# A chunk of weights folded in halves around the second stage, and other chunks' bit work moved behind the steps' copies

## The chip, the core and the metric

The kernel runs on one core of a Trainium2 chip. The metric is the device time of one execution in microseconds. A core has five engines that run side by side, each in its own program order: TensorE (PE) multiplies matrices into PSUM banks, VectorE (DVE), ScalarE (ACT) and GpSimd (POOL) work elementwise, and SyncE (SP) issues most of the DMAs. They wait for one another through semaphores.

## The reference, cut to what matters

```python
def _attn_ref(x):                       # x: (8, 3008, 256)
    X = np.fft.fft(x, axis=1)
    X = np.fft.fft(X, axis=2)
    return X.real.astype(np.float32)

def _moe_ref(x, w_in, w_out):           # w_in (256, 2048), w_out (2048, 256)
    h = x @ w_in
    g = h * (1.0 / (1.0 + np.exp(-1.702 * h)))
    return (g @ w_out).astype(np.float32)
```

The real part of a two-dimensional Fourier transform of each of 8 batches goes through a two-layer network with a sigmoid-type activation. Everything is 32-bit floats.

## The kernel before

The transform along the sequence is split into two stages of matrix products (3008 = 47 x 64). The transform along the 256 features is never done by itself: it is folded into the first weight matrix, `wcs = cd x w_in`, in four chunks of 512 columns (`fold_w(0)` to `fold_w(3)`). The network then runs in 384 steps (8 batches x 3 blocks x 2 halves x 8 pairs of 128 hidden columns). The first eight steps (`t < NP`, NP = 8) go through `hidden`, `rows`, `activate` and, three steps later (`LAG = 3`), `product`; all later ones go through `begin`, `forward`, `backward` and others. Steps 0 and 1 need chunk 0 of the folded weights, steps 2 and 3 chunk 1, and so on.

The weights do not arrive as plain floats: w_in and w_out come as 64-bit words whose bits are turned into 32-bit floats on the chip. Each of the eight chunks, named `("in", n)` or `("out", n)` (`in0`, `in1`, `out0`, `in2` and so on in the text), is loaded into a ring of three raw buffers and goes through these operations, each over 128 x 1024 elements:

- `prepare` takes a buffer each of the rings `s`, `m` and `r`;
- `squares` (L401, ScalarE; for chunk `in0` L403, VectorE) squares the high word, read as a float;
- `clamp` (L406, GpSimd) limits it;
- `low_up` (L411) and `low_down` (L416), both ScalarE, round the low word;
- `high` (L433, L434, L435, VectorE) masks and shifts the clamped word into a buffer of ring `a`;
- `finish_in` (L447, GpSimd) or `finish_out` (L455, two instructions) adds both parts, into `wst` or `wo`.

`bounds(key)` is prepare, squares, clamp, low_up and low_down in a row. A raw buffer is free for the load three places later once its clamp, squares and low_up are done: `load_in(3)` follows `out0`, `load_out(2)` follows `in2`, and `load_out(3)` follows `out1` in that ring.

`fold_w(n)` multiplies both halves of `wst[n]` (i = 0, 1) into two PSUM banks and ScalarE copies them to `wcs` (L474). `first_row(n)` makes two small per-column factors of the chunk by eight tiny products and two ScalarE copies (L482, L483). `rotate` (psr, with a copy at L341) and `stage2` (L354, then VectorE's transposes L360) make the operand `pq` of block 0. `nyquist(0, 0)` makes the row `nb` by a product and a ScalarE copy (L372). `warm` issues a matmul with no use of its result.

In step t < 8, `hidden(t)` multiplies `pq` with two pairs of columns into banks `pa` and `pb`, and ScalarE copies `pa` to `v` (L515); `rows(t)` makes the hidden rows on VectorE (L553, L556 twice, L544); `activate(t - 1)` is one ScalarE instruction (L562).

Program order is the order of each engine: the kernel schedules by hand. Before the steps stands a list of calls; within the steps the dictionary `extra` holds what runs at the end of step t, entered with `at(t, function, ...)`. PSUM banks without a fixed name are handed out in rotation from the list `spare` (six tags); a bank's next user waits for its last reader. At t = NP - 3 = 5, `hidden` takes `b0` and `b1` by name.

The SP queue holds, in order: `load_in(3)` (L383), `load_out(2)` and `load_out(3)` (L388), `load_matrices` (L318), `turn` (L194, L190: part of the next batch is reversed into a DRAM buffer Xr), `load_x` (L203: the next batch, half of it from Xr), and two 4 KB DMAs of zeros into row 0 of `wcs[1]` (L970). The first of these zeros is needed by `begin(8, 1)`, the product into `x` with which TensorE opens step 8.

Of the kernel before, what the change touches and what calls it, by code (L numbers as in the profile page):

```python
# [111 lines left out]
def kernel(ctx: ExitStack, tc, x, w_in, w_out, tab1, tab2, out):  # L112
# [36 lines left out]
    o_banks = [psp.tile([128, 512], F32, tag=f"o{i}", name=f"o{i}") for i in range(2)]  # L149
    rest = psu.enter_context(tc.tile_pool(name="psu", bufs=1, space=PS))  # L150
    big = cv.tile([128, 19 * 1024], F32, tag="big", name="big")
    rings = {"s": (0, 1024, 3), "a": (3072, 1024, 1), "raw": (4096, 2048, 3), "h": (10240, 1024, 4), "r": (14336, 1024, 2),
             "m": (16384, 1024, 2)}
    turns = {}

# [11 lines left out]
    def bank(name, tag=None):  # L167
        if tag is None:
            tag = spare.pop(0)
            spare.append(tag)  # L170
        if tag in ("o0", "o1"):
            return o_banks[int(tag[1])]
        return (rest if tag[0] == "o" else psp).tile([128, 512], F32, tag=tag, name=name)
# [5 lines left out]
    def halves(out, lhs, rhs, **how):  # L179

        for c0 in (0, 64):
            nc.tensor.matmul(out[c0:c0 + 64], lhsT=lhs[:, c0:c0 + 64], rhs=rhs, skip_group_check=True, **how)  # L182
# [137 lines left out]
    def warm(n):  # L320

        ps = bank("warm")
        for _ in range(n):
            nc.tensor.matmul(ps[:], lhsT=wcs[0][:, 0:128], rhs=wcs[0][:, 0:512], start=True, stop=True)
# [11 lines left out]
    def rotate(b, a0=0, a1=NG, copy=None):  # L336

        col = t4t[b][:, a0:a1, H]
        ps = bank("psr")
        halves(ps[:, 0:a1 - a0], rot, col, start=True, stop=True)  # L340
        (copy or nc.vector.tensor_copy)(col, ps[:, 0:a1 - a0])  # L341
# [51 lines left out]
    def prepare(key):  # L393


        pre[key] = ring("s"), ring("m"), ring("r").bitcast(U32)

    def squares(key, eng):
        g, hi = pre[key][0], raw[key][:, :, 1].bitcast(F32)
        if eng is nc.scalar:  # L400
            eng.activation(g[:], hi, ACTF.Square)  # L401
        else:
            eng.tensor_tensor(g[:], hi, hi, op=ALU.mult)  # L403

    def clamp(key, lo=0, n=1024):
        nc.gpsimd.tensor_scalar(pre[key][1][:, lo:lo + n], raw[key][:, lo:lo + n, 1].bitcast(F32), scalar1=TOP, scalar2=-TOP,  # L406
                                op0=ALU.min, op1=ALU.max)

    def low_up(key, lo=0, n=1024):

        nc.scalar.activation(pre[key][2][:, lo:lo + n].bitcast(F32), raw[key][:, lo:lo + n, 0], ACTF.Copy, scale=2.0 ** -29,  # L411
                             bias=2.0 ** 23)
# [12 lines left out]
    def high(key, lo=0, n=1024):  # L425

        g, m, _ = (t[:, lo:lo + n] for t in pre[key])
        bits = m.bitcast(U32)
        if lo == 0:
            made_a[key] = ring("a").bitcast(U32)  # L430
        a = made_a[key][:, lo:lo + n]
        dve = nc.vector
        dve.scalar_tensor_tensor(m, g, LOW * LOW, m, op0=ALU.is_ge, op1=ALU.mult)  # L433
        dve.tensor_scalar(a, bits, scalar1=3, scalar2=0x3FFFFFF8, op0=ALU.logical_shift_left, op1=ALU.bitwise_and)  # L434
        dve.scalar_tensor_tensor(a, bits, 0xC0000000, a, op0=ALU.bitwise_and, op1=ALU.bitwise_or)  # L435
# [5 lines left out]
    def finish_in(n, lo=0, k=1024):  # L441

        if lo == 0:
            wst[n] = op.tile([128, 2, 512], F32, tag="os", name="wst")
        key, part = ("in", n), slice(lo, lo + k)
        out = wst[n][:].rearrange("p i f -> p (i f)")[:, part]
        nc.gpsimd.tensor_tensor(out.bitcast(U32), made_a[key][:, part], pre[key][2][:, part], op=ALU.add)  # L447
# [16 lines left out]
        for out, i0, i1 in ((t1, b12, b11), (t2, b22, t1), (t3, b22, b12), (t4, b21, t2)):  # L464
            nc.gpsimd.tensor_tensor(out, i0, i1, op=ALU.subtract)

    def fold_w(n):
        ps = [bank("psw") for _ in range(2)]
        for i in range(2):
            for cs in range(2):  # L470
                halves(ps[cs][:], cd[:, i, cs, :], wst[n][:, i, :], start=(i == 0), stop=(i == 1))
        for cs in range(2):

            nc.scalar.copy(wcs[cs][:, n * 512:(n + 1) * 512].rearrange("p (f c) -> p f c", f=4),  # L474
                           free(ps[cs][:], 0, [1, 4], [4, 128]))
# [400 lines left out]
        spill_first(k, 16, NM, (nc.sync, nc.sync))  # L876
    prepare(in1)
    squares(in1, nc.scalar)
    for h0 in (0, 512):
        finish_in(0, h0, 512)  # L880
    clamp(in1)
    low_up(in1)
    low_down(in1)
    high(in1)
    load_out(1, nc.sync)
    fill(0, 4, NG)
    warm(1)
    fold_w(0)
    warm(1)
    first_row(0)  # L890
    prepare(out0)
    finish_in(1)
    clamp(out0)
    rotate(0, 0, 4, nc.scalar.copy)
    squares(out0, nc.scalar)
    stage2(0, 0)
    warm(1)
    low_up(out0)
    low_down(out0)
    high(out0)  # L900
    load_in(3, nc.sync)
    prepare(in2)
    squares(in2, nc.scalar)
    clamp(in2)
    fold_w(1)
    finish_out(0)

    extra, early = {}, {}

    def at(t, fn, *args):  # L910
        extra.setdefault(t, []).append((fn, args))

    n = len(steps)

    for t, key in (1, in2), (2, ("out", 1)), (3, ("in", 3)), (5, ("out", 2)), (6, ("out", 3)):
        at(t, high, key)
        if key != in2:
            at(t - 1, bounds, key)
        at(t + 1, finish, key)
    early[3], early[5] = 2, 3  # L920
    rows_at = {1: 1, 4: 2, 6: 3}
    for t, c in ((0, 2), (1, 3)):
        at(t, load_out, c, nc.sync)
    at(3, load_matrices)
    if B > 1:
# [35 lines left out]
    for t in range(n + LAG):  # L961
        if t < NP:
            if t == NP - 3:
                spare[:] = [tag for tag in spare if tag[0] == "o"] + ["b2"]
            hidden(t)
            if t == NP - 1:
                middle(NP)
                begin(NP)
                for c0 in range(0, DF, 1024):
                    nc.sync.dma_start(out=wcs[1][0:1, c0:c0 + 1024], in_=tab1[127:128, n0 + 4:n0 + 1028])  # L970
            if t == 0:
                low_up(in2)
                nyquist(0, 0)
                low_down(in2)
            if t in rows_at:
                first_row(rows_at[t])
            if t >= LAG:
                product(t - LAG, 0, None)
            if t in early:
                fold_w(early[t])  # L980
            if t:
                activate(t - 1)
            rows(t)
            if t == NP - 1:
                doubled(NP)
                middle(NP + 1)
        else:
            after, special = (any(fn in (mix1, stage2) for fn, _ in extra.get(k, ())) for k in (t - 1, t))
            if t < n:
                begin(t, 1)  # L990
            if t == NP:
                activate(t - 1)
            if t < n:
                forward(t)
            if after and t + 1 < n:
                middle(t + 1)
            opening = (t - LAG) % NP == 0 and t >= NP + LAG
            one, other = (t - LAG, (1, 2, 4, 7)), (t - LAG - 1, (5, 6, 3))
            if opening:
                small_products(*other)  # L1000
            cut = 0 if opening and not after else 3 if after else 2
            product(t - LAG, 0, cut)
            if after:
                small_products(one[0], one[1][:1])
                small_products(other[0], () if opening else other[1][:1])
            if t + 1 < n:
                begin(t + 1)
            if not opening:
                small_products(other[0], other[1][after:])
            product(t - LAG, cut, 6 if t - LAG == last else None)  # L1010
            small_products(one[0], one[1][after:])
            swap(t - LAG - 2)
            if t < n:
                backward(t)
            if t + 1 < n:
                doubled(t + 1)
            if t < n:
                activate_back(t)
                sums(t, nc.gpsimd)
            if t + 2 < n and not special:  # L1020
                middle(t + 2)
            combine_small(t - LAG - 1)
            if t - LAG == last:
                product(last, 6, None)
            sums(t - 1, nc.vector)
            deeper(t - 2, 0)
            deeper(t - 3, 1)
        if t == NP:
            psu.close()
            low = ctx.enter_context(tc.tile_pool(name="low", bufs=1, space=PS))  # L1030
            pot["low"] = low.tile([128, 3 * 512], F32, tag="low", name="low")
        if t >= LAG:
            combine(t - LAG)
            combine_last(t - LAG - 2)
            turn_last(t - LAG - 3, 0)
            turn_last(t - LAG - 4, 1)
        if t >= NP:
            spare[:] = [f"b{t % 2}"] * special + ["b2"]
        for fn, args in extra.get(t, ()):
            fn(*args)  # L1040
# [28 lines left out]
```

## Time and profile before

| | us |
|---|---|
| median of 4 runs | 1866.89 (1864.21 to 1868.07) |
| device time of the profiled execution | 1861.57 |
| its span, first to last instruction | 1859.8 |
| TensorE busy in 0 to 25 us | 22.38 |
| in 25 to 36 us (11 us) | 8.92 |
| in 36 to 48, 48 to 60, 60 to 72 us (12 us each) | 12.00, 10.72, 12.00 |
| in 72 to 85 us (13 us) | 11.91 |
| bytes moved in 36 to 48, 48 to 60, 60 to 72, 72 to 85 us | 343, 342, 172, 123 GB/s |

The granted TensorE clock is 1.00 in all these stretches. In the lines of a timeline the first number is the start and the second the duration in microseconds; in brackets stands how long the engine was idle before, and what ended it. A record of 8 or 16 instructions on one line is one run of equal instructions. The DMA share of the stretch from 36 to 60 us is 0.97 to 1.03, from 60 to 85 us 0.82 to 0.86, and from 85 to 97 us 0.01.

### The profile page before, as it was taken

How to read it: one execution, taken by the hardware profiler on the slowest of the kernel's cores; microseconds unless marked ns; L12 is line 12 of the kernel's file. 1: busy time of each engine (PE TensorE's matmuls, PEld its weight loads, DVE VectorE, ACT ScalarE, POOL GpSimd, SP SyncE). 2: the span in 40 equal slices, each digit the busy share in tenths (PEclk: the TensorE clock that was granted, in tenths of full speed). 3: DMA queues.
4: the chain of work that ended last, by engine and by line, in shares of the span. 5: the costliest groups of instructions: out<-in, count | busy, mean ns of one | idle time of the engine just before them, and what ended most of it. 6: DMA issues, size and time to landing. Idle time of an engine off the chain costs nothing.

```text
span 1859.8 us, 55818 instructions
## 1 busy us (share of the span) xinstructions
PE 1843.4 (99%) x23684; PEld 1404.8 (76%) x23684; DVE 1522.7 (82%) x2229; ACT 1149.9 (62%) x2248; POOL 963.4 (52%) x1057
## 2 busy tenths in 40 slices
PE   8999999999999999999999999999999999999998
PEld 5677777777777777777777777777777777778776
DVE  7888788888798877997789878888888888878874
ACT  6656656666656656666665666656666666656663
POOL 5676346744367444773347643476445754434442
PEclk9999999999999999999999999999999999999999
DMA  8720351125120350114402152022511021100111
GB/s 278 181 52 17 83 95 35 30 63 108 24 51 14 82 95 18 51 21 107 68 13 57 39 103 49 18 59 50 104 30 25 19 63 36 31 19 13 22 20 24
DMA packets 145690, 105.29 MB, mean 57 GB/s; under 512 B 105163, under 2 KB 128235, under 8 KB 144258
## 3 DMA queue, kind: packets, MB, share of 16 engines
q1 hardware_dynamic: 144226, 101.20, 25.3%
q8 instruction: 187, 3.06, 0.7%
q10 hardware_dynamic: 1216, 0.52, 0.1%
q14 instruction: 61, 0.50, 0.1%
HBM read 64.41 MB, written 48.05 MB: 60 GB/s over the span
## 4 chain that ended last, share of the span: by engine, by line
PE 87%; DVE 6%; ACT 3%; DMA 2%; POOL 1%; issue 1%; SPq 0%; DVEq 0%; ACTq 0%; POOLq 0%
PE x L182 32%; PE o L182 24%; PE low L664 23%; PE o L664 4%; DVE big L630 2%; PE ps L354 1%; PE ps L253 1%; DVE big L765 1%; DVE big L544 1%; DMA wcs<-in_tab_dram 1%; ACT x L571 1%; DMA big<-in_moe_w_in_dram 1%; ACT big L586 0%; ACT xt L256 0%; ACT g L583 0%
## 5 line engine op out<-in xcount | busy, mean ns | idle before, releaser
L601 POOL TENSOR_TENSOR big<-big 128x256 f32<-128x256 f32 (+1 forms) x376 | 349.6, 930 | 840.5 <-ACT big L593 790.0
L182 PE MATMUL x<-pq,wcs 128*64 128x256 f32 (+1 forms) x6016 | 771.4, 377 | 3.6 <-ACT g L583 2.2
L630 DVE TENSOR_TENSOR big<-big 128x512 f32<-128x512 f32 (+1 forms) x736 | 636.6, 879 | 30.9 <-PE low L664 14.0
L182 PE MATMUL o<-big,wo 128*64 128x256 f32 (+1 forms) x4800 | 621.1, 375 | 0.0
L182 PEld LDWEIGHTS x<-pq,wcs 128*64 128x64 f32 x6016 | 410.0, 137 | 193.8 <-issue 15.6
L182 PEld LDWEIGHTS o<-big,wo 128*64 128x64 f32 x4800 | 341.8, 137 | 146.7 <-DVE big L608 0.5
L583 ACT ACTIVATE g<-x 128x512 f32<-128x512 f32 (+1 forms) x376 | 221.6, 589 | 372.7 <-PE x L182 371.5
L544 DVE TENSOR_TENSOR big<-g,x 128x512 f32<-128x512 f32 (+2 forms) x440 | 253.7, 588 | 200.5 <-ACT big L586 200.1
L664 PE MATMUL low<-big 128*64 128x128 f32 (+1 forms) x5888 | 381.9, 270 | 0.0
L571 ACT ACTIVATE x<-nb,af 128x256 f32<-128x256 f32 (+1 forms) x752 | 352.7, 469 | 12.2
L664 PEld LDWEIGHTS low<-big 128*64 128x64 f32 x5888 | 337.1, 137 | 28.7
L602 POOL TENSOR_TENSOR big<-big 128x256 f32<-128x256 f32 (+1 forms) x376 | 358.6, 954 | 0.0
L586 ACT ACTIVATE big<-x 128x512 f32<-128x512 f32 (+1 forms) x376 | 220.5, 586 | 196.4 <-PE x L182 180.5
L593 ACT ACTIVATE big<-big 128x512 f32<-128x512 f32 (+1 forms) x376 | 231.8, 617 | 41.8 <-DVE big L544 40.0
L664 PE MATMUL low<-big,wo 128*64 128x128 f32 (+1 forms) x2944 | 220.2, 270 | 0.2 <-DVE big L630 0.2
L664 PEld LDWEIGHTS low<-big,wo 128*64 128x64 f32 x2944 | 171.9, 137 | 3.8 <-DVE big L630 0.4
L609 DVE TENSOR_TENSOR big<-big 128x512 f32<-128x512 f32 (+1 forms) x188 | 147.7, 786 | 6.5
L608 DVE TENSOR_TENSOR big<-big 128x512 f32<-128x512 f32 (+1 forms) x188 | 136.6, 727 | 5.4 <-POOL big L601 5.4
L765 DVE TENSOR_TENSOR big<-big,low 128x512 f32<-128x512 f32 (+3 forms) x184 | 109.0, 609 | 3.5
L664 PEld LDWEIGHTS o<-big,wo 128*64 128x64 f32 x1472 | 92.3, 137 | 24.9
L664 PE MATMUL o<-big,wo 128*64 128x128 f32 (+1 forms) x1472 | 110.1, 270 | 0.0
L225 POOL TENSOR_TENSOR xt<-xt 111x510 f32<-111x510 f32 x56 | 77.1, 1377 | 4.4
(102 smaller groups left out, 965.2 us busy)
## 6 DMA issues: line engine op xcount, KB each, us to landing
out_dram<-os SPq DMA_DIRECT2D x284, 64.0 KB
t<-Td SPq DMA_DIRECT2D x22, 512.0 KB
Td<-xt SPq DMA_DIRECT2D x14, 768.0 KB
xt<-in_x_dram SPq DMA_DIRECT2D x14, 512.0 KB
xt<-Xr SPq DMA_DIRECT2D x14, 512.0 KB
nb<-Nd SPq DMA_DIRECT2D x23, 256.0 KB
out_dram<-os SPq DMA_DIRECT2D x96, 56.0 KB
Xr<-in_x_dram SPq DMA_DIRECT2D x7, 752.0 KB
```

Of the source, the lines that this page charges most:

```text
L182: nc.tensor.matmul(out[c0:c0 + 64], lhsT=lhs[:, c0:c0 + 64], rhs=rhs, skip_group_check=True, **how)
L544: nc.vector.tensor_tensor(free(out, at + m - 1, [by, 2], [RUN, blocks], [-1, m]), *ins, op=op)
L571: nc.scalar.activation(x[:, i * 256:i * 256 + n], nbt[b, blk][:, hh * 256:hh * 256 + n], ACTF.Copy, scale=af1[:, f:f + 1])
L583: nc.scalar.activation(two(g[:], n), two(xb[t][:], n), ACTF.Copy, scale=2.0)
L586: nc.scalar.activation(front(t), two(xb[t][:], width(t)), ACTF.Gelu_apprx_sigmoid)
L593: nc.scalar.activation(back(t), back(t), ACTF.Gelu_apprx_sigmoid)
L601: eng.tensor_tensor(right(t, S1, n), left(t, A21, n), right(t, A22, n), op=ALU.add)
L602: eng.tensor_tensor(left(t, S3, n), left(t, A11, n), left(t, A21, n), op=ALU.subtract)
L608: eng.tensor_tensor(s2, s1, a11, op=ALU.subtract)
L609: eng.tensor_tensor(s4, a12, s2, op=ALU.subtract)
L630: nc.vector.tensor_tensor(out, i0, i1, op=how)
L664: nc.tensor.matmul(o, lhsT=lhs, rhs=rhs, start=first_in, stop=(p == NP - 2), skip_group_check=True)
```

## The change

`fold_w` can now do one half at a time; the chain of clamp, finish and fold of chunk `in1` is cut into halves, and `fold_w(1)` is placed around `rotate` and `stage2`. Two of the three `warm(1)` calls ahead of the steps are left out. `low_up` and `low_down` of `out0`, and `squares`, `low_up` and `low_down` of `in2`, move into steps 0 and 1; `finish_out(0)` and `finish(in2)` move to the end of step 1, the bounds of `out1` from step 1 to step 2, and `load_out(2)` and `load_out(3)` each one step later. Ring `a` of masked words has two buffers instead of one, ring `s` two instead of three.

```diff
-    rings = {"s": (0, 1024, 3), "a": (3072, 1024, 1), "raw": (4096, 2048, 3), "h": (10240, 1024, 4), "r": (14336, 1024, 2),
+    rings = {"s": (0, 1024, 2), "a": (2048, 1024, 2), "raw": (4096, 2048, 3), "h": (10240, 1024, 4), "r": (14336, 1024, 2),
...
-    def fold_w(n):
-        ps = [bank("psw") for _ in range(2)]
-        for i in range(2):
+    folded = {}
+
+    def fold_w(n, parts=(0, 1)):
+        if parts[0] == 0:
+            folded[n] = [bank("psw") for _ in range(2)]
+        ps = folded[n]
+        for i in parts:
             for cs in range(2):
                 halves(ps[cs][:], cd[:, i, cs, :], wst[n][:, i, :], start=(i == 0), stop=(i == 1))
+        if parts[-1] == 0:
+            return
...
     squares(in1, nc.scalar)
-    for h0 in (0, 512):
-        finish_in(0, h0, 512)
+    finish_in(0, 0, 512)
     clamp(in1)
+    finish_in(0, 512, 512)
     low_up(in1)
     low_down(in1)
-    high(in1)
+    for h0 in (0, 512):
+        high(in1, h0, 512)
     load_out(1, nc.sync)
     fill(0, 4, NG)
     warm(1)
     fold_w(0)
-    warm(1)
+    prepare(out0)
+    for h0 in (0, 512):
+        finish_in(1, h0, 512)
+    clamp(out0)
+    fold_w(1, (0,))
+    rotate(0, 0, 4, nc.scalar.copy)
+    stage2(0, 0)
+    squares(out0, nc.scalar)
+    fold_w(1, (1,))
     first_row(0)
-    prepare(out0)
-    finish_in(1)
-    clamp(out0)
-    rotate(0, 0, 4, nc.scalar.copy)
-    squares(out0, nc.scalar)
-    stage2(0, 0)
-    warm(1)
-    low_up(out0)
-    low_down(out0)
     high(out0)
-    load_in(3, nc.sync)
     prepare(in2)
-    squares(in2, nc.scalar)
     clamp(in2)
-    fold_w(1)
-    finish_out(0)
...
-    for t, key in (1, in2), (2, ("out", 1)), (3, ("in", 3)), (5, ("out", 2)), (6, ("out", 3)):
+    at(1, finish_out, 0)
+    at(1, high, in2)
+    at(1, finish, in2)
+    at(2, bounds, ("out", 1))
+    for t, key in (2, ("out", 1)), (3, ("in", 3)), (5, ("out", 2)), (6, ("out", 3)):
         at(t, high, key)
-        if key != in2:
+        if t > 2:
             at(t - 1, bounds, key)
         at(t + 1, finish, key)
...
-    for t, c in ((0, 2), (1, 3)):
+    for t, c in ((1, 2), (2, 3)):
         at(t, load_out, c, nc.sync)
...
             if t == 0:
-                low_up(in2)
                 nyquist(0, 0)
-                low_down(in2)
+                low_up(out0)
+                load_in(3, nc.sync)
+            if t == 1:
+                low_down(out0)
             if t in rows_at:
                 first_row(rows_at[t])
+            if t == 1:
+                squares(in2, nc.scalar)
+                low_up(in2)
+                low_down(in2)
```

## The prediction

> **What bounds the kernel now.** I read four views, in this order. The page first: TensorE is busy 99% of the span.
>
> ```profile
> PE 1843.4 (99%) x23684; PEld 1404.8 (76%) x23684; DVE 1522.7 (82%) x2229; ACT 1149.9 (62%) x2248; POOL 963.4 (52%) x1057
> ```
>
> The edit touches only what runs before step 8 of 384, so its effect is how far it moves the matmul at 84.73 us, with which step 8's turn begins; all later work is TensorE-bound and shifts with it. Second, the TensorE timeline up to there.
>
> ```profile
> 35.92 3.65 PE L182 MATMUL psw<-wst,small 128*64 128x512 f32 x16 [0.97 <-POOL wst L447]
> 39.41 1.03 PE L182 MATMUL pa<-pq,wcs 128*64 128x256 f32 x8
> ...
> 48.20 3.65 PE L182 MATMUL o<-big,wo 128*64 128x256 f32 x32
> ...
> 80.85 3.65 PE L182 MATMUL o<-big,wo 128*64 128x256 f32 x32
> 84.73 0.98 PE L182 MATMUL x<-pq,wcs 128*64 128x226 f32 x8 [0.23 <-DMA wcs<-in_tab_dram]
> ```
>
> The second chunk's fold (35.92) stands ahead of the first step (39.41), which does not use that chunk. Product 0 follows at 48.20. At 84.73 TensorE waits 0.23 us for a DMA. The chain of waits says which (start, length, what):
>
> ```profile
> 64.68 0.57 SPq L203
> ...
> 69.73 14.86 DMA wcs<-in_tab_dram
> 84.59 0.14 issue
> 84.73 0.98 PE x L182 x8
> ```
>
> A 4 KB row of zeros is issued at 69.73 and lands at 84.59, behind the loads of the next batch. Third, the waits of the DMA-issuing queue say what holds those loads.
>
> ```profile
> SPq L203 <- DMA Xr<-in_x_dram: 5.0, 1, 5.0
> SPq L388 <- ACT big L411: 4.8, 1, 4.8
> ```
>
> Load 3 of w_out (L388, issued at 48.17) waits for ScalarE's low_up of `out1`. Everything after it is one queue: matrices, the turns into Xr, the batch loads (which wait for Xr until 64.5), the zeros. So two paths meet at step 8: TensorE's, ready at about 84.5, and the DMA queue's, 84.59. Moving one alone gains nothing.
>
> Fourth, the timelines of the three other engines where the edit works. ScalarE: the copy nb, activate 0, and the copy v of step 2:
>
> ```profile
> 42.35 0.59 ACT L372 COPY nb<-psn 128x512 f32<-128x512 f32 x1 [0.22 <-PE psn L182]
> ...
> 44.91 1.06 ACT L562 ACTIVATE big<-big 128x1024 f32<-128x1024 f32 x1
> ...
> 49.10 0.57 ACT L515 COPY v<-pa 128x512 f32<-128x512 f32 x1
> ```
>
> GpSimd's clamp of `out1` and finish of `in2`:
>
> ```profile
> 44.95 1.23 POOL L406 TENSOR_SCALAR big<-big 128x1024 f32<-128x1024 f32 x1 [1.19 <-DMA big<-in_moe_w_out_dram]
> 50.04 2.37 POOL L447 TENSOR_TENSOR wst<-big 128x1024 uint32<-128x1024 uint32 x1 [3.86 <-DVE big L435]
> ```
>
> The end of row 4 on VectorE:
>
> ```profile
> 62.63 0.86 DVE L556 SCALAR_TENSOR_TENSOR dif<-nb,af,pb 128x256 f32<-128x256 f32 x2
> 63.53 0.69 DVE L544 TENSOR_TENSOR big<-pa,dif 128x512 f32<-128x512 f32 x1
> ```
>
> [...]4 KB took 14.86 us. [...]The trace: the batch loads released at 64.5 start to move bytes at about 66.0, so 1.5 us before data. [...]L434 on 128x1024 takes 0.69 us alone, 1.54 beside a clamp. [...]The trace has gaps to 0.97 us and a clock of 1.00 throughout.
>
> **The change part by part.** Steps are walked with start-to-start times of before.
>
> *Fold 1 earlier.* The two spare warm matmuls go (1 us each, both inside TensorE waits: nothing). VectorE's `high(in1)` starts when clamp and squares are in, 27.7 instead of 30.15 (the clamp now stands ahead of the second finish), in halves: 1.9 to 2.2 us each, ends about 32. GpSimd finishes the halves (1.28 each) at about 31.2 and 33.4. TensorE: fold 0 ends 30.8; first half of fold 1 31.25 to 33.0 (half of 3.49); psr 0.22 and stage 2 1.08 (32.52, 32.74, 33.82 were their starts and end) to 34.3; second half 1.75 to 36.05; first_row 0.56 (44.12 to 44.72 before); step 0 at 36.6. Its bank needs ScalarE's copy of fold 1, behind squares(out0), whose DMA lands at 34.87: 34.87+1.05+0.59 = 36.5. So step 0 starts at 36.65, 2.75 us earlier. VectorE's high(out0), 36.05 to about 39.5, is in time for row 0.
>
> *ScalarE gives it back.* The copy nb comes 2.94 us after step 0's start: 39.59. Between it and activate 0 there were low_down, a v copy and two small copies (44.91-42.35 = 2.56). Now there are low_up and low_down of `out0` and all three operations of `in2`: 0.49 (nb) + 1.06 (low_up) + 0.46 (v) + 0.95 (low_down) + 0.12 (small copies) + 1.06 + 1.22 + 0.96 (squares, low_up, low_down of `in2`) = 6.32, all spacings of the same operations before. Activate 0 runs 45.91 to 46.97 and product 0 starts at 47.0, where TensorE would have been ready at 36.65 + (48.20-39.41) = 45.4. Left: 1.2 of 2.75 us. finish_out(0) runs 42.7 to 45.2, in time.
>
> *Bounds of `out1` a step later.* v of step 2 at 46.86, activate 1, then out1 and in3 in one run of 2 x 3.24: v of step 3 at 54.75 against 54.87. The copies of fold 2 stand behind it, 55.2 and 55.7, so step 4 starts at 55.85 against 55.97: nothing left. TensorE idles from 54.0.
>
> *A bank changes hands.* Two bank takes fewer before the steps shift the rotation, and step 5 takes b0 by name. In the order of the built kernels its first matmul now waits on VectorE and ScalarE, before only on TensorE: it is row 4's bank. Row 4 ended at 64.22 and step 5 started at 62.73. Rows 3 and 4 are up to 1.3 us earlier, as v 3 comes at 55.3 and high(out1) ends at 55.1 to 56.4. So step 5 starts at 62.9 to 64.27: 0.2 to 1.5 us late. From there to product 4 the chain is as before: TensorE ready for step 8 at 84.7 to 86.0.
>
> *The w_out loads wait longer.* Load 2 now waits for low_up(in2): 39.59+4.14+1.18 = 44.9, not 42.21. It is hidden: out1, fill and in3, about 1.05 MB each, move from about 40.6, where DMA activity takes up again after a hole, and last to 49.0 at the 374 GB/s shown for 42 to 48. Load 3 waits for low_up(out1), 46.86+0.46+0.95+1.06+1.16 = 50.5, and for clamp(out1), which now stands behind finish(in2): high(in2) ends about 47.6, finish 50.0, clamp 51.2. Issue at 51.3 instead of 48.17, 3.1 us later. Before, its bytes could start at 40.6+4.2/0.375 = 51.8, behind four loads; [...]matrices, turns, batch loads and zeros follow. Zeros land at 85.6 to 86.1. I take 86.0.
>
> *Sum.* Step 8's matmul starts 0.14 after the later of 86.0 and 84.7 to 86.0, at 86.15: +1.4 us. On the profiled execution the span 1859.8 becomes 1861.2 and the device time 1861.57, with its 1.8 us around the span, 1863.0. That execution is 5.3 us below the median 1866.89; the shift is the same on both: 1868.3. The second buffer for masked words lets L434 start before the finish of the chunk before is done; that wait ended 0.02 to 0.1 us of each trio, so I count nothing. Ring s with two buffers waits only on words consumed two chunks earlier. If these covers fail, VectorE is late by at most one finish, 2.5 us, inside the next case.
>
> **The rivals.**
> *The gain goes through*: step 0's 2.75 us reaches the end, 1864.1. For it: TensorE is 99% busy. Against: it needs the zeros 2.75 us earlier, and nothing moves their queue forward.
> *Nothing moves*: the backlog hides load 3 altogether and TensorE is ready by 84.6, 1866.9. For it: in3 landed only at 51.65 before[...]. Against: the bank wait.
> *Slower: the queue's whole delay counts.* Load 3's issue slips with no cover from the backlog, or the clamp is contended (52.38 took 2.13 us, not 1.23) after a contended high(in2) (4.05 us at 37.02). Issue then falls at 52.6, 4.4 us late, and the zeros land at 89.0: +4.3 us, 1871.2. It decides once the bytes of load 3 begin after 55.5. For it: SP is in order and every later load stands behind. Against: the 7 us from 41 to 48 in which the DMA rows show no hole.
>
> **How the numbers follow.** Forecast 0.56, own range 1866.5 to 1870; gain through 0.12; nothing moves 0.10; queue's whole delay 0.22. A measurement here tells 0.2% (3.7 us) from no change. The median's runs scatter by 1.9 us each way. Slower: three quarters of 0.22 and an eighth of 0.56, 0.23. Faster: the 2.75 us lie below the bound, so a fifth of 0.12, 0.03. The rest, 0.74, is same. The range: 1864.0 (gain through) to 1872.5 (whole delay, and scatter).
>
> **What would show it.** Step 0's first pa matmul near 36.7, product 0 near 47.0 waiting on ScalarE's activate, step 4 near 55.9 behind fold copies, step 5 waiting on VectorE's row 4, load 3 of w_out issued after 51 behind GpSimd's clamp, and step 8 waiting for the zeros at about 86.1. Zeros landing at 84.6, or a step 8 earlier than 84, would make the prediction wrong; so would a clock below 1.00 beside TensorE's gap of 1.9 us before step 4.

## The result and the profile after

| | before | after |
|---|---|---|
| median, us | 1867.04 (1861.54 to 1869.41, 63 runs) | 1869.38 (1863.33 to 1874.16, 44 runs) |
| profiled execution: device time, span, us | 1861.57, 1859.8 | 1870.78, 1868.9 |

The ratio is 1.0016, with an interval of 1.0010 to 1.0022: the change costs about 3 us (1.9 to 4.1), near the bound of what can be told.

The two profiled spans differ by 9.1 us, and most of that isn't the change. The first chunk of weights landed 2.12 us later in the second execution: VectorE's L403, which waits for it and which no edit touches, started at 22.81 instead of 20.69 (in the other traces of changed kernels between 19.44 and 22.67). And what follows step 8's first product took 1775.1 us before and 1779.5 after (span less that start). With the kernel before_zeros below, whose code from there on is that of before, it took 1779.9, and over all traces shown here 1775.1 to 1782.7: so this part varies between executions. Therefore all times below, unless called absolute, are counted from L403's start, and the measure is the start of step 8's `x` product. Between the changed kernel and a second profile of it, this measure repeats to 0.15 us.

| us after L403 | before | after |
|---|---|---|
| fold 0, its two halves | 5.91, 8.35 | 5.89, 9.47 |
| fold 1 | 15.23 (whole) | 12.20, 15.22 (halves) |
| step 0, first `pa` product | 18.72 | 17.64 |
| product 0 | 27.51 | 28.17 |
| step 4 | 35.28 | 36.91 |
| product 1 | 38.45 | 39.89 |
| step 5 | 42.04 | 45.05 |
| step 8, `x` product | 64.04 | 66.58 |

By this measure the change costs 2.54 us. It wins 1.08 at step 0, and by product 0 that is lost. TensorE's timeline of the changed kernel, in absolute times (start, length; in brackets the idle time before and what ended it), shows where:

```profile
28.70 1.94 PE L182 MATMUL psw<-wst,small 128*64 128x512 f32 x8 [1.00 <-POOL wst L447]
32.28 1.94 PE L182 MATMUL psw<-wst,small 128*64 128x512 f32 x8 [1.63 <-POOL wst L447]
35.01 1.94 PE L182 MATMUL psw<-wst,small 128*64 128x512 f32 x8 [0.80 <-POOL wst L447]
...
40.45 1.08 PE L182 MATMUL pa<-pq,wcs 128*64 128x256 f32 x8
...
50.98 3.67 PE L182 MATMUL o<-big,wo 128*64 128x256 f32 x32 [1.43 <-ACT big L568]
...
59.72 1.08 PE L182 MATMUL pa<-pq,wcs 128*64 128x256 f32 x8 [1.46 <-ACT wcs L480]
...
67.86 1.08 PE L182 MATMUL pa<-pq,wcs 128*64 128x256 f32 x8 [1.41 <-DVE t L341]
...
85.94 3.65 PE L182 MATMUL o<-big,wo 128*64 128x256 f32 x32
89.39 0.96 PE L182 MATMUL x<-pq,wcs 128*64 128x226 f32 x8
```

Three stalls stand where before had none: 1.43 us for activate 0 (L568), 1.46 for the copies of fold 2 (L480), and 1.41 for row 4, whose bank step 5 now takes. For the last one the view names L341, a small VectorE copy that follows row 4; the last reader of the bank, row 4's L550, ended at 67.71, just ahead of it. In return step 8 no longer waits for a DMA. In the kernel before, the second half of fold 0 and step 5 stood like this:

```profile
29.04 1.94 PE L182 MATMUL psw<-wst,small 128*64 128x512 f32 x8 [0.50 <-POOL wst L447]
...
62.73 1.06 PE L182 MATMUL pa<-pq,wcs 128*64 128x256 f32 x8
```

The halves of fold 0 lie 3.58 us apart, against 2.44 before. The timeline of all engines around them in the changed kernel says why:

```profile
27.56 1.38 DVE L434 TENSOR_SCALAR big<-big 128x512 uint32<-128x512 uint32 x1
...
28.62 1.33 POOL L406 TENSOR_SCALAR big<-big 128x1024 f32<-128x1024 f32 x1
...
28.97 1.53 DVE L435 SCALAR_TENSOR_TENSOR big<-big 128x512 uint32<-128x512 uint32 x1
...
30.65 1.57 POOL L447 TENSOR_TENSOR wst<-big 128x512 uint32<-128x512 uint32 x1 [0.70 <-DVE big L435]
31.14 1.37 DVE L434 TENSOR_SCALAR big<-big 128x512 uint32<-128x512 uint32 x1
```

The clamp of `in1` now runs ahead of the second finish, and VectorE's L435 beside it took 1.53 us instead of 0.69. The finish of the second half waits for that L435, and `high(in1)` starts behind it. VectorE's timeline of before has the same two instructions; L434 ran beside a finish there too, L435 alone:

```profile
25.46 1.38 DVE L434 TENSOR_SCALAR big<-big 128x512 uint32<-128x512 uint32 x1
...
26.87 0.69 DVE L435 SCALAR_TENSOR_TENSOR big<-big 128x512 uint32<-128x512 uint32 x1
```

ScalarE's timeline of the changed kernel, from nb to activate 0 and to the v copy of step 3:

```profile
43.45 0.59 ACT L372 COPY nb<-psn 128x512 f32<-128x512 f32 x1 [1.28 <-PE psn L182]
...
49.79 1.04 ACT L568 ACTIVATE big<-big 128x1024 f32<-128x1024 f32 x1
...
55.39 1.15 ACT L401 ACTIVATE big<-big 128x1024 f32<-128x1024 f32 x1
56.44 1.18 ACT L411 ACTIVATE big<-big 128x1024 f32<-128x1024 uint32 x1
57.65 1.06 ACT L416 ACTIVATE big<-big 128x1024 uint32<-128x1024 f32 x1
58.61 0.57 ACT L521 COPY v<-pa 128x512 f32<-128x512 f32 x1
59.08 1.08 ACT L480 COPY wcs<-psw 128x512 f32<-128x512 f32 x2
```

ScalarE works without a gap from nb on. From nb to that v copy it takes 15.16 us (12.52 before); nb is 1.02 earlier, so v 3 and step 4 are late by 2.64 - 1.02 = 1.62. The chain of waits of the changed kernel (start, length, what) runs over the other two engines instead:

```profile
50.78 1.24 DVE big L435
...
52.17 2.38 POOL wst L447
54.55 1.17 POOL big L406
55.72 0.02 issue
55.74 2.17 DVE big L433
...
59.81 0.68 DVE big L559
```

Finish(in2), then clamp(out1), then high(out1), then row 3 at 59.81. ScalarE's v 3 ended at 59.18, only 0.6 us earlier: two chains of nearly equal length reach the same place. That matters for the repairs below.

The queue of the w_out loads, from SP's timeline: loads 2 and 3, on one line.

```profile
48.87 7.21 SPq L388 DMA_DIRECT2D big<-in_moe_w_out_dram  x2
```

Load 3 was issued at about 55.7, which is 32.9 after L403, where before it was 27.5: 5.4 us later. The zeros still landed before TensorE asked for them, since step 8 shows no wait.

### The profile page after: what moved, and what is told of

The parts are those of the page before. It is cut to its first block, busy times and chain, and to the rows that moved or that the text cites. A ratio compares the mean times of both kernels' runs of the same rounds, so it can differ in the third digit from the quotient of the medians.

```text
span 1868.9 us, 55815 instructions
## 1 busy us (share of the span) xinstructions
PE 1842.8 (99%) x23680; PEld 1424.2 (76%) x23680; DVE 1526.0 (82%) x2232; ACT 1150.2 (62%) x2248; POOL 962.4 (51%) x1058
## 4 chain that ended last, share of the span: by engine, by line
PE 86%; DVE 7%; ACT 3%; POOL 1%; issue 1%; DMA 1%; SPq 0%; DVEq 0%; ACTq 0%; POOLq 0%
PE x L182 32%; PE o L182 24%; PE low L670 23%; PE o L670 4%; DVE big L636 2%; PE ps L354 1%; PE ps L253 1%; DVE big L771 1%; DVE big L550 1%; ACT x L577 1%; DMA big<-in_moe_w_in_dram 1%; DVE big L433 1%; DMA wo<-in_tab_dram 0%; ACT big L592 0%; DVE big L614 0%
## 5 line engine op out<-in xcount | busy, mean ns | idle before, releaser
L182 PEld LDWEIGHTS x<-pq,wcs 128*64 128x64 f32 x6016 | 419.9, 137 | 185.6 <-issue 15.5
L182 PEld LDWEIGHTS o<-big,wo 128*64 128x64 f32 x4800 | 350.3, 137 | 141.3 <-POOL wo L455 1.9
L550 DVE TENSOR_TENSOR big<-g,x 128x512 f32<-128x512 f32 (+2 forms) x440 | 253.8, 588 | 202.6 <-ACT big L592 202.1
L670 PEld LDWEIGHTS o<-big,wo 128*64 128x64 f32 x1472 | 93.7, 137 | 23.8 <-issue 0.2
```

Source lines behind the costliest of these rows:

```text
L550: nc.vector.tensor_tensor(free(out, at + m - 1, [by, 2], [RUN, blocks], [-1, m]), *ins, op=op)
L670: nc.tensor.matmul(o, lhsT=lhs, rhs=rhs, start=first_in, stop=(p == NP - 2), skip_group_check=True)
```

## The experiments

Three theories. A: the engines' own chain (clamp, ScalarE's order, the bank) sets step 8. B: the queue of zeros behind the late load 3 sets it. C: idle stretches of TensorE cost clock. Line numbers are up to three higher in kernels with the zeros edit.

**again**: the changed kernel a second time, to see how far its trace repeats.

> The changed kernel itself, unaltered, as the yardstick of the others. I measure in the trace the stretch from the start of VectorE's square of the first chunk (L403, begun when that chunk has landed) to the first x product of step 8: 64.04 us before the change (20.69 to 84.73), 66.58 us after it (22.81 to 89.39). Both theories expect 66 to 67 us again, and 2 to 3 us over the kernel before. Theory A (the engines): step 8 is held by TensorE's own chain, pushed by ScalarE, the clamp and the bank of step 5. Theory B (the queue, as in the prediction): step 8 is held by the zeros that stand behind the late load 3 of w_out; then step 8 shows a wait for the DMA in some executions.

Ratio 1.0022, interval 1.0013 to 1.0031. Step 0 at 17.66, step 4 at 36.94, step 5 at 45.19, step 8 at 66.73: the table's loss is no accident of one execution.

**bank_turned**: the rotation of PSUM banks is turned by two, as before had it.

```diff
     fold_w(0)
+    spare[:] = spare[2:] + spare[:2]
     prepare(out0)
```

> The rotation of the PSUM banks is turned on by two, so that step 5 no longer takes the bank of row 4. Theory A: the first product of step 5 starts some 1.4 us sooner after the rotate product (no wait for VectorE), and step 8 up to 1.4 us sooner, 65.2 us in the stretch. Theory B: step 5 starts sooner too, but step 8 then waits for the zeros: the last bytes of the batch loads moved at about 87.1 us in the changed kernel, and in the kernel before the zeros landed 1.4 us after them, so about 88.5, and the gain is limited to 0.9 us.

Ratio 1.0015, interval 1.0004 to 1.0025. TensorE's timeline of bank_turned:

```profile
65.53 1.06 PE L182 MATMUL pa<-pq,wcs 128*64 128x256 f32 x8
...
83.63 3.65 PE L182 MATMUL o<-big,wo 128*64 128x256 f32 x32
89.64 0.98 PE L182 MATMUL x<-pq,wcs 128*64 128x226 f32 x8 [2.36 <-DMA wcs<-in_tab_dram]
```

Step 5 no longer waits and starts at 43.51 instead of 45.05: the bank's price is 1.5 us, shown. TensorE is free for step 8 2.36 us before it starts, at 65.26, but the zeros are not there: 67.62. That is 1.04 later than in the changed kernel, where both theories expected it earlier. So A sets the changed kernel's time and B stands right behind. By the DMA rows the bytes ahead of the zeros moved until about 66.5, in the changed kernel until about 65.0, although nothing in the queue's order differs. Most of that delay is already there when the first load from Xr goes out, 47.63 after L403 (69.65 absolute) against 46.42 (69.23); what made the turns into Xr late is left open.

**bank_zeros, before_zeros**: the first DMA of zeros goes ahead of `load_matrices`; once on bank_turned, once on the kernel before.

```diff
+    def clear(c0):
+        nc.sync.dma_start(out=wcs[1][0:1, c0:c0 + 1024], in_=tab1[127:128, n0 + 4:n0 + 1028])
...
+    at(3, clear, 0)
     at(3, load_matrices)
...
-                for c0 in range(0, DF, 1024):
-                    nc.sync.dma_start(out=wcs[1][0:1, c0:c0 + 1024], in_=tab1[127:128, n0 + 4:n0 + 1028])
+                clear(1024)
```

> The banks turned by two as before, and the first 4 KB of zeros issued after step 3's work, ahead of the matrices, the turns and the batch loads (the second stays where it is). In the run with the banks turned alone, TensorE had finished product 4 at 87.1 us and waited 2.36 us for the zeros (stretch from L403 to step 8: 67.62 us). Theory B (the queue of zeros holds what the bank gives back): the wait goes and the stretch is 65.1 us, 1.6 us less than the changed kernel and still 1.0 us more than the kernel before. Theory A alone (the wait is an accident of that execution): the stretch is the same 65.1 us, but the timed median then stands no better against the run with banks turned alone.

> The kernel before with the first 4 KB of zeros issued after step 3's work, ahead of the matrices, the turns and the batch loads. In its profile TensorE was ready for step 8 at 84.5 us and the zeros landed at 84.59. Both theories: the stretch from L403 to step 8 is 63.8 us instead of 64.04 where the DMA queue was on time; if in other executions the zeros come later than TensorE, as they vary by a microsecond from run to run, the timed median gains up to 1 us. More than 1.5 us would say that the zeros held the kernel before in most executions.

In bank_zeros step 8 starts at 65.04 with no wait, ratio 1.0005 (0.9993 to 1.0018). In before_zeros it starts at 63.75, 0.29 earlier than before, with its 0.23 us wait gone, ratio 1.0009 (0.9997 to 1.0021). The queue is removed from the path in both. Turning the banks and moving the zeros so takes 66.58 - 65.04 = 1.5 us out of the changed kernel. What is left over before_zeros is 65.04 - 63.75 = 1.3 us, all from the engines; the timed ratios can't resolve it.

**clamp_behind**: clamp(in1) goes back behind the second finish.

```diff
     finish_in(0, 0, 512)
-    clamp(in1)
     finish_in(0, 512, 512)
+    clamp(in1)
```

> The clamp of the second w_in chunk goes back behind the second finish of the first chunk. Theory A: the second half of fold 0 starts about 1 us sooner against the first half (3.58 us apart in the changed kernel, 2.44 before it), as L435 is no longer slowed to 1.53 us by the clamp and the finish does not stand behind it; step 0 and step 8 follow by up to 1 us. Theory B: step 0 earlier, but step 8 gains at most what load 3 gains in issue time, as far as the zeros hold it. If the clamp's place were without effect, the two halves stay 3.6 us apart.

Ratio 1.0041, interval 1.0028 to 1.0054. The halves of fold 0 are 2.42 apart again (5.89, 8.31), with L435 back at 0.69 us: the 1.53 us came with the clamp beside it. But the clamp itself now comes later, TensorE idles, and the forecast gain of up to 1 us at step 0 does not come: something new happens. TensorE's timeline of clamp_behind, and its windows (stretch, length, busy of PE, PEld, DVE, ACT, POOL, then the granted clock, DMA share, GB/s):

```profile
30.80 1.94 PE L182 MATMUL psw<-wst,small 128*64 128x512 f32 x8 [0.49 <-POOL wst L447]
35.55 3.62 PE L182 MATMUL psw<-wst,small 128*64 128x512 f32 x8 [2.81 <-POOL wst L447]
```

```profile
33.60:35.50 1.90, 0.00 (x0) 0.00 (x0) 1.86 (x3) 0.00 (x0) 1.57 (x1) 1.00 0.95 395
35.50:37.30 1.80, 1.75 (x4) 0.53 (x6) 0.97 (x2) 0.00 (x0) 0.71 (x1) 0.52 1.02 403
37.30:39.10 1.80, 1.80 (x10) 0.57 (x6) 0.00 (x0) 0.00 (x0) 1.77 (x3) 0.53 1.05 394
39.10:41.00 1.90, 1.90 (x74) 1.28 (x72) 0.64 (x2) 1.27 (x2) 1.01 (x1) 1.00 1.02 369
```

After 2.81 us of idle time the same eight matmuls took 3.62 us instead of 1.94, at half the clock; step 0 slips to 20.19. So this run alone doesn't price the clamp.

**clamp_warm, clamp_warm2**: the same, with one or two warm matmuls behind fold 0.

```diff
     fold_w(0)
+    warm(2)
```

> The clamp of the second w_in chunk behind the second finish, as in the earlier run of that kind, and one warm matmul put back between fold 0 and fold 1. In that run TensorE idled 2.81 us there, the granted clock then read 0.52 to 0.58 for about 3.8 us and the first half of fold 1 took 3.62 us instead of 1.94; step 0 began 20.19 us after L403. Theory C (the idle stretch costs the clock, and a warm matmul keeps it): the first half of fold 1 takes 1.94 us again and step 0 begins at about 18.5 us. Otherwise it takes 3.6 us again.

> The kernel clamp_behind with two warm-up matmuls behind fold 0 in place of clamp_warm's one. If the idle TensorE is what costs the clock (theory C), and one warm matmul left too long an idle stretch behind it, the granted clock stays near 1.00 until fold 1, the first half of fold 1 takes 1.94 us and step 0 starts near 18.5 us after L403's start (20.19 and 20.12 without and with one). If the slow stretch comes from elsewhere, it takes 3.3 to 3.6 us again and step 0 stays near 20.1.

The extra call also turns the bank rotation, so only times up to step 0 are compared. One warm matmul didn't help: the half fold took 3.32 us after an idle time of 1.74, step 0 at 20.12. Two did, in TensorE's timeline of clamp_warm2:

```profile
32.09 1.98 PE L324 MATMUL warm<-wcs 128*128 128x512 f32 x4
34.97 1.94 PE L182 MATMUL psw<-wst,small 128*64 128x512 f32 x8 [0.89 <-POOL wst L447]
```

Idle 0.89 us, 1.94 us for the half, clock 1.00, step 0 at 18.51, as theory C said. Now the two prices part: the clock 20.19 - 18.51 = 1.68 us in the profiled executions, and the clamp behind the second finish 18.51 - 17.64 = 0.87. The change's own place for the clamp is the better one, contention and all.

**bounds_back**: the bounds of `out1` back at step 1, ahead of finish(in2), and load 3 with them.

```diff
+    at(1, bounds, ("out", 1))
     at(1, finish, in2)
-    at(2, bounds, ("out", 1))
...
-    for t, c in ((1, 2), (2, 3)):
+    for t, c in ((1, 2), (1, 3)):
```

> The bounds of the second w_out chunk go back to the end of step 1, ahead of the finish of the third w_in chunk, and load 3 of w_out follows them there. Theory A: ScalarE has only one set of bounds between the copies v of steps 2 and 3, so v 3 and step 4 come about 2 us sooner against activate 0 (step 4 began 9.93 us after activate 0 in the changed kernel), while step 3 and row 2 come later as v 2 stands behind the bounds; step 8 gains 0.5 to 1.5 us. Theory B: load 3 is issued about 4 us sooner, the hole in the DMA share (0.72 from 48 to 60 us) closes, and step 8 moves with the zeros, 1.5 to 2.5 us sooner.

Ratio 1.0021, interval 1.0009 to 1.0034. Step 4 at 36.99 (36.91), step 8 at 66.67 (66.58). v 2 is later (31.24 for 27.93), v 3 the same (35.88 for 35.80): ScalarE does the same sum of work before v 3 in either order. So theory A's forecast for this run, step 4 about 2 us sooner, missed. Load 3 goes out about 2.6 us earlier, and step 8 does not move: B is no part of the changed kernel's loss, and its forecast missed too.

**refit**: bank_zeros, and on ScalarE low_up(out0) ahead of nb's copy, squares(in2) before the steps, the rest of `in2` behind activate 0.

```diff
     prepare(in2)
+    squares(in2, nc.scalar)
     clamp(in2)
...
-                nyquist(0, 0)
                 low_up(out0)
+                nyquist(0, 0)
...
-            if t == 1:
-                squares(in2, nc.scalar)
-                low_up(in2)
-                low_down(in2)
...
                 activate(t - 1)
+            if t == 1:
+                low_up(in2)
+                low_down(in2)
```

> Banks turned, zeros first, and ScalarE's work placed where it idled: low_up of the first w_out chunk ahead of the copy nb (ScalarE sat idle 1.28 us there), squares of the third w_in chunk ahead of the first copy v, and its low_up and low_down behind activate 0 instead of ahead of it. Theory A: activate 0 starts about 2.0 us after nb instead of 6.3, product 0 no longer waits for it and starts about 2 us sooner than in the changed kernel (26.2 us after L403 instead of 28.2, before the change 27.5); v of step 3 and step 4 about 2 us sooner, near 35 us after L403; step 8 at 63 to 64 us. If ScalarE's order is not what delays product 0 and step 4, they stay at 28.2 and 36.9 us.

Ratio 1.0005, interval 0.9993 to 1.0018. Product 0 comes at 27.15 with no wait (28.17). ScalarE's order was that stall. But step 4, expected near 35, is at 37.90, later than the 36.96 of bank_zeros. ScalarE's timeline of refit:

```profile
52.99 1.18 ACT L404 ACTIVATE big<-big 128x1024 f32<-128x1024 f32 x1 [2.06 <-DMA big<-in_moe_w_in_dram]
...
56.23 0.57 ACT L524 COPY v<-pa 128x512 f32<-128x512 f32 x1
56.70 1.08 ACT L483 COPY wcs<-psw 128x512 f32<-128x512 f32 x2
```

ScalarE now reaches squares(in3) before that chunk has landed, waits 2.06 us, and v 3 and the fold copies stand behind it. Step 8, expected at 63 to 64, is at 65.48. In this trace the first chunk landed early (L403 at 19.44) and fold 0 had to wait for TensorE, so step 0 is at 18.05 against 17.65 in bank_zeros: about 0.4 us of these times belongs to that execution.

**refit2**: refit, with `in3`'s three operations moved behind the v copy, the fold copies and activate 2 in step 3, and clamp(out1) ahead of finish(in2). **refit3**: refit2 with that clamp behind finish(in2) again.

```diff
     at(1, high, in2)
+    at(1, prepare, out1)
+    at(1, clamp, out1)
     at(1, finish, in2)
...
                 activate(t - 1)
+            if t == 3:
+                squares(in3, nc.scalar)
+                low_up(in3)
+                low_down(in3)
```

> The kernel refit, with the third input chunk's squares, low_up and low_down moved on ScalarE from ahead of the v copy of row 3 to behind that copy, behind the copies of fold 2 and behind activate 2, and with clamp(out1) ahead of finish(in2) on GpSimd. If ScalarE's order with the late load of that chunk was what held refit, product 0 stays near 27.2 us after L403's start with no wait, step 4 comes to about 36.3 (37.90 in refit), step 5 to about 42.2 and step 8 to about 63.8 (65.48 in refit, 66.6 in the changed kernel). If the chain lies elsewhere, step 4 stays near 37.9 and step 8 near 65. The measured ratio can't tell these apart: between 0.999 and 1.001.

> The kernel refit2 with clamp(out1) put back behind finish(in2) on GpSimd. In refit2 that clamp ran beside high(in2), whose first two instructions took 1.98 and 1.64 us (1.22 and 0.69 alone), and fold 2 waited 2.28 us for finish(in2). If that contention is what is left, fold 2 starts near 30.9 us after L403's start (32.39 in refit2), step 4 near 34.5 (35.87), product 1 near 38.2 (39.04) and step 8 near 63.4 (64.17; 64.04 in the kernel before), so about 0.6 us earlier than before by the trace, which the measured ratio cannot resolve (0.999 to 1.001). If the row behind high(out1) holds product 1, step 8 stays near 64.2.

refit2: product 0 at 26.46, step 4 at 35.87, step 8 at 64.17, ratio 1.0007 (0.9993 to 1.0020). This run has two edits, but refit3, which takes the clamp back, has step 4 at 34.96: so it is ScalarE's order that held step 4 in refit. With the clamp ahead, VectorE's L434 of high(in2) (L437 in this kernel) ran beside it and took 1.64 us (0.69 in refit, with GpSimd idle beside it), and fold 2 waited 2.28 for its finish. The L433 ahead of it took 1.98, and 1.74 in refit, where no clamp ran beside it, so most of that is not the clamp's doing. refit3 missed its expectation (63.4): step 8 at 66.24, ratio 1.0006 (0.9994 to 1.0018). TensorE's timeline of refit3:

```profile
52.12 3.65 PE L182 MATMUL psw<-wst,small 128*64 128x512 f32 x16 [1.33 <-POOL wst L450]
55.60 1.08 PE L182 MATMUL pa<-pq,wcs 128*64 128x256 f32 x8
56.51 1.03 PE L182 MATMUL pb<-pq,wcs 128*64 128x256 f32 x8
59.58 0.93 PE L182 MATMUL psf<-twos,wcs 1*64 1x1 f32 x16 [2.04 <-DVE big L553]
60.44 4.98 PE L182 MATMUL o<-big,wo 128*64 128x256 f32 x32
```

Fold 2 and step 4 come earlier (31.48, 34.96), but psf in front of product 1 waits 2.04 us for row 3, which stands behind high(out1) and its clamp: the second of the two chains. Product 1 starts at 39.80, where the changed kernel had 39.89, and then takes 4.98 us instead of 3.67. Without that and psf's 0.3 us more, step 8 would have come at about 64.6, still behind before. The windows of refit3 show the clock at half once more:

```profile
57.80:59.60 1.80, 0.02 (x2) 0.05 (x2) 1.76 (x5) 1.77 (x3) 1.80 (x2) 1.00 1.08 204
59.60:61.40 1.80, 1.80 (x22) 1.41 (x24) 1.77 (x2) 1.80 (x5) 0.39 (x1) 0.53 0.94 238
61.40:63.20 1.80, 1.80 (x12) 1.04 (x10) 1.77 (x3) 1.80 (x3) 0.00 (x0) 0.52 1.05 373
63.20:65.00 1.80, 1.80 (x20) 1.16 (x18) 1.77 (x4) 1.77 (x2) 1.77 (x1) 1.00 1.08 383
```

No version beats the kernel before by a measurable amount; the earliest step 8 in a trace is before_zeros with 63.75.

## Why the prediction was right, and where not

The total held: 1868.3 was forecast, 1869.38 came. The shift itself was put too small: +1.4 us stands against 3 us (1.9 to 4.1) by the ratio and 2.54 by the traces. And the sum was put together otherwise than forecast. The wait for the zeros that was to set the end did not come; in its place stood a gain at step 0 that fell short by 1.67 us and passed on to TensorE's own chain. That the total came so near is partly luck.

- **Fold 1 earlier** is the step that failed in size. It gave step 0 2.75 us, measured are 1.08. The two halves of fold 1 were put at 10.56 and 13.61 after L403 and came at 12.20 and 15.22. Three durations were too short: L435 of `in0` beside the clamp took 1.53 us, not 0.69, so high(in1) started at 7.61, not 7.0; its first half took 2.81 us, not 1.9 to 2.2, because L434 beside GpSimd takes 1.37 (0.43 alone); and the finish beside the next L434 took 1.58, not 1.28. Together 0.6 + 0.75 + 0.3, which is the 1.64 us. Each instruction was costed without the neighbour that its new place gives it, although the trace of before held such a price (L434 at 25.46, 1.38 us). The second half of fold 0, 1.12 us later than before, was not in the forecast; it cost nothing, as TensorE waited another 0.80 us behind it. The clamp's place is right all the same: clamp_warm2 puts it at 0.87 us in favour.
- **ScalarE gives it back** held: activate 0 came 49.79 - 43.45 = 6.34 us after nb (6.32 forecast). refit showed the cause by removing it.
- **Bounds of `out1` a step later**: v 3 was forecast at 15.16 us after nb and came at 15.16. "Nothing left" of the gain became a loss of 1.63 us at step 4, since nb was only 1.02 us earlier instead of 2.76 (42.35 - 39.59).
- **A bank changes hands**: right in kind, 1.5 us by bank_turned. Step 5 was put 0.2 to 1.5 us late and came 3.0 late; the 1.67 us that step 0 lacked are in that difference.
- **The w_out loads wait longer**: load 3 went out 5.4 us later, not 3.1, as everything ahead of it on GpSimd and ScalarE was late. The bytes ahead of the zeros moved until about 65.0 after L403, before until about 63.0, so the zeros landed later too, but step 8 didn't wait for them: with TensorE ready at 66.58, not at 64.0 to 65.3, the wait that the forecast put last was hidden. (The forecast's 86.0 for the zeros was the author's estimate. With the 1.5 us from release to first byte that the trace of before shows at 64.5, load 3's bytes start at 51.3 + 1.5 = 52.8, 1.0 us later than before, and the zeros land at 85.6; anything later was not shown. In the changed kernel load 3's first byte moved about 1.0 us after its issue at 55.7.) That step named the wrong holder for the changed kernel; bank_turned shows that it is the next in line.
- **The clock beside a gap before step 4**: the gap was 1.46 us and the clock stayed at 1.00 there.

Of the rivals, "the gain goes through" and "nothing moves" fall. The slower one, "queue's whole delay", at 1871.2 is not much farther from the measured time than the forecast, but its mechanism is not what happened: bounds_back moved load 3 forward and nothing came of it.

## What to carry to other kernels

Before an operation is moved to another place on one engine, look at what it will then run beside on the others: here instructions slowed by their neighbour on another engine took about 1.6 of the forecast 2.75 us. When work is only put in another order on an engine that has no gap, a stall moves to whoever is now behind it, so follow each moved group to its last dependent (here v, the fold copies and the activate). And when two chains of nearly equal length meet, move both in one experiment, or the second hides what the first gave.

## What the runs showed of the hardware

**The clock.** Three kernels had TensorE at half clock for a while before step 8, each time behind a gap. By slices of 0.4 us the granted clock stood at 0.50 from 35.58 to 38.98 absolute in clamp_behind, behind a gap of 2.81 us; from 59.72 to 63.13 in refit3, behind 2.04; and from 34.59 to 38.01 in clamp_warm, behind 1.74: about 3.41 us each time. The half folds there took 3.62 us (clamp_behind) and 3.32 (clamp_warm) instead of 1.94, and product 1 of refit3, mostly inside its stretch, 4.98 instead of 3.67.

Gaps of 2.28 us (before fold 2 of refit2) and 2.37 (before step 4 of refit) were followed by work at full speed: the fold behind the first took 3.65 us and the product behind the second 1.08, both as in the changed kernel. A gap's length alone does not decide, then; what does, these runs do not show.

**VectorE beside GpSimd.** L434 is not the only instruction that took longer beside GpSimd. L435 on 128x512 took 1.53 us beside the clamp (changed kernel, at 28.97) and 0.69 alone (before, at 26.87). L433 on 128x1024 took 2.16 beside a clamp (changed kernel, at 55.74) and 1.23 alone (before, at 30.15). The forecast had not counted the first of these.
